# K and V caches loaded by groups of partitions instead of groups of heads

## The chip, the cores and the metric

The kernel runs on one core of one Trainium2 chip. The metric is the device time of one execution in microseconds. The kernel before took 277.62, 280.21 and 280.53 us in three runs, so its median is 280.21 us. The profile is of one more execution, of 279.63 us.

## The reference: what is computed

One decode step of an attention block beside a GEGLU feed-forward block, and its backward pass: the output and the gradients of x, both caches and all weights. The attention looks at the last W = 1024 positions of the caches only. Shapes: B = 4 sequences, one query position each, D = 512, 32 query heads, 8 kv-heads, a cache of 4096 positions, head size 128, F = 1792, all in bfloat16.

```python
xn = _layernorm(x)
q = (xn @ wq).reshape(B, 1, 32, 128).transpose(0, 2, 1, 3)
k = jnp.repeat(k_cache[:, :, Sk - W:, :], 4, axis=1)      # W = 1024 of Sk = 4096
v = jnp.repeat(v_cache[:, :, Sk - W:, :], 4, axis=1)
p = _softmax(jnp.einsum("bhqd,bhkd->bhqk", q, k) * 128 ** -0.5)
o = jnp.einsum("bhqk,bhkd->bhqd", p, v)
out = x + o.transpose(0, 2, 1, 3).reshape(B, 1, 4096) @ wo + (_gelu(xn @ w_gate) * (xn @ w_up)) @ w_down
# returned: out, and the vjp of it for grad_out in x, k_cache, v_cache, wq, wo, w_gate, w_up, w_down
```

The gradients of the caches have the full shape (4, 8, 4096, 128). Their first 3072 positions are zero, and the kernel has to write these zeros.

## The kernel before

**Memory traffic.** Of 111.88 MB that the DMA engines move, the loads into the on-chip memory SBUF (128 partitions) are 30.68 MB: the weights, and for each of the four sequences one K tile and one V tile of 2 MB. The stores are 81.01 MB. 32 stores of 1.5 MB write the zeros of the cache gradients, all from one constant tile `ztile` (function `zeros`, L278). The rest are results: 16 stores of 1 MB for the last 1024 positions of dK and dV, and the weight gradients.

**Queues.** Every load and every store of zeros is issued by SyncE (SP), in the order of the program; the transfers of one issuer form one queue (q1), which each of the 16 DMA engines works off in order. The result stores are issued by GpSimd (POOL) on a queue of its own (q0, function `result`, L113). `zeros(n)` lets at most four stores of zeros be under way at once. The compiled program also gives SP's transfers eight semaphores in turn, so a transfer waits to be issued until the one eight issues before it has landed.

**Order on SP's queue.** Weights; K of sequence 0; three stores of zeros; V of sequence 0; 2 zeros; K of 1; 4 zeros; V of 1; 2 zeros; K of 2; 3 zeros; V of 2; 2 zeros; K of 3; 3 zeros; V of 3; 13 zeros; two small outputs. K alternates between two buffers, `ka` and `kb`. V has a single buffer `va`, so V of sequence b + 1 is issued (L698) only when the matmuls of `od(0, b)` (L597) have read V of b. Below, K0 to K3 and V0 to V3 are the tiles of the sequences.

**How a tile lies.** `load_kv` (L258) makes a tile of [128 partitions, 8 kv-heads, 8, 128]. Partition m holds, of each kv-head, the positions 8m to 8m + 7 of the window. So for one partition and one head the source is a run of 8 x 128 x 2 = 2,048 bytes, and the heads lie 1 MB apart.

**Who reads a tile.** `score` (L528) transposes a tile on VectorE (DVE) in four steps of 128x1024 through `t32` (L92); each step reads all 128 partitions and every second kv-head (`src[:, g2:G:2, ...]`, L537), and matmuls on TensorE (PE, through `mm`, L136) follow. `score(0, b + 1, n)` for K of the next sequence is spread over the second half of the loop over b; `score(1, b, n)` for V of this one stands at its head. `od` (L597) then reads all partitions of the tile.

**The loop over sequences** (L643) holds the softmax, its backward pass and the matmuls for dK and dV (units of `dvdk`, L570, handed out by `move`, L121; their results go through `stg` tiles, L102, to the result stores). After it come the output projection (L737) and the weight gradients of wo and wq (from L749).

The calls of `load_kv` in the loop, with the zeros behind them (L697 to L699 and L718 to L720):

```python
                if b + 1 < B:
                    load_kv(b + 1, 1, att, "va", nc.sync)
                    zeros((2, 2, len(ztodo))[b])
...
                if b + 2 < B:
                    load_kv(b + 2, 0, (kap, att)[b % 2], ("ka", "kb")[b % 2], nc.sync)
                    zeros(3)
```

Of the kernel before, what the change touches and what calls it, by code (L numbers as in the profile page):

```python
# [15 lines left out]
P = 128  # L16
# [3 lines left out]
def kernel(  # L20
# [27 lines left out]
    _, G, Sk, Dh = A_k_cache.shape  # L48
# [4 lines left out]
    K0 = Sk - W  # L53
    F = B_w_gate.shape[1]
    Q = 32
# [5 lines left out]
    J = W // P  # L61
# [196 lines left out]
    def load_kv(b, k, pool, tag, eng, **kw):  # L258
        d_, src = ((k_t, A_k_cache), (v_t, A_v_cache))[k]
        tl = pool.tile([P, G, J, Dh], BF16, name=tag, tag=tag)  # L260
        for hf in range(2):
            hs = slice(hf * G // 2, (hf + 1) * G // 2)
            with tc.high_priority():
                d = eng.dma_start(out=tl[:, hs].rearrange("p g j d -> p g (j d)"),
                                  in_=src[b, hs, K0:Sk, :].rearrange("g (m j) d -> m g (j d)", j=J), **kw)
        d_[b] = tl
        return d

# [22 lines left out]
    if True:  # L291
# [15 lines left out]
        nc.sync.dma_start(out=wq_sb[:].rearrange("p c n -> p (c n)"), in_=A_wq.rearrange("(p c) n -> p (c n)", c=C))  # L307
        nc.sync.dma_start(out=wo_sb[:].rearrange("p k n -> p (k n)"), in_=A_wo.rearrange("(p k) n -> p (k n)", k=KH))
        load_kv(0, 0, kap, "ka", nc.sync)
        zeros(3)  # L310

# [117 lines left out]
    with tc.tile_pool(name="mid", bufs=1, reuse_waits="tile") as mid:  # L429
# [3 lines left out]
        selb = mid.tile([Q, 4, P], BF16, name="selb")  # L433
        with tc.tile_pool(name="att", bufs=1, reuse_waits="tile") as att:
            load_kv(0, 1, att, "va", nc.sync)
            zeros(2)
            load_kv(1, 0, att, "kb", nc.sync)
            zeros(4)

# [127 lines left out]
            def small(name, shape=(P, 1)):  # L567
                return att.tile(list(shape), FP32, name=name, tag=name)
# [74 lines left out]
            for b in range(B):  # L643
                S = sps[0][:]
                m = small("m")
# [249 lines left out]
```

## Time and profile before

| | |
|---|---|
| median of three runs | 280.21 us (277.62 to 280.53) |
| profiled execution | 279.63 us, its span 277.9 us |
| PE, DVE, ACT, POOL busy | 63%, 64%, 44%, 18% of the span |
| q1 (issued by SP) | 13,944 packets, 81.02 MB, 71.1% of 16 DMA engines' span |
| q0 (issued by POOL) | 6,368 packets, 30.67 MB, 27.2% |
| DMA parts of the chain that ended last | 30% of the span, 22% of it on `va` |
| `va` transfers, 1 MB each, issue to landing (median) | 14.6 us |
| `ka` and `kb` transfers, 1 MB each, issue to landing (median) | 24.5 and 21.6 us |
| stores of zeros, 1.5 MB each, issue to landing (median) | 20.9 us |

The span runs from the first instruction to the last. A share of DMA time adds the time that the packets took and divides it by 16 engines' span; packets of one engine overlap a little, so it can pass 100% in a short stretch. Time from issue to landing includes the wait behind older transfers of the same queue.

### The profile page before, as it was taken

The page shows a single profiled execution, that of the slowest core. Times are in us where ns is not written, and L with a number is a line of the kernel's source. Part 1 is how long each engine was busy: PE and PEld are TensorE (multiplying, and loading weights), DVE is VectorE, ACT ScalarE, POOL GpSimd, SP SyncE. Part 2 cuts the span into 40 slices and gives each one's busy share as a digit, 9 for nine tenths or more (in the row PEclk, how much of TensorE's full clock was granted, in tenths as well). Part 3 has the DMA queues.
Part 4 walks back from the last instruction along what each step waited for, and adds up shares of the span by engine and source line. Part 5 has one row for each costly group of instructions (what it writes and reads, how often), then busy time and mean ns, then how long its engine had stood idle before and what let it go on. Part 6 is the DMA issues. An engine that isn't in the chain of part 4 may idle for free.

```text
span 277.9 us, 3158 instructions
## 1 busy us (share of the span) xinstructions
PE 174.9 (63%) x1095; PEld 57.7 (21%) x1095; DVE 177.0 (64%) x331; ACT 122.0 (44%) x247; POOL 50.6 (18%) x121
## 2 busy tenths in 40 slices
PE   1257988868347857986430987631987366897560
PEld 0112432123023411331000323101332001122010
DVE  7789679889787198738321736713718376665980
ACT  2244676730202475847150644540646257353470
POOL 8500100285152013310200100200200202010110
PEclk9985985559755555575555555555555557555555
DMA  7999989999999999999999999999999999999686
GB/s 263 435 472 416 410 337 427 425 426 402 430 403 433 429 403 424 409 429 424 394 416 428 409 421 424 396 417 432 431 417 426 409 417 406 413 392 408 270 333 246
DMA packets 20335, 111.88 MB, mean 403 GB/s; under 512 B 1360, under 2 KB 1376, under 8 KB 14688
## 3 DMA queue, kind: packets, MB, share of 16 engines
q1 hardware_dynamic: 13944, 81.02, 71.1%
q0 software_dynamic: 6368, 30.67, 27.2%
q8 instruction: 8, 0.13, 0.2%
q14 instruction: 7, 0.06, 0.0%
q10 hardware_dynamic: 8, 0.00, 0.0%
HBM read 30.68 MB, written 81.01 MB: 402 GB/s over the span
## 4 chain that ended last, share of the span: by engine, by line
DMA 30%; PE 23%; DVE 9%; ACT 5%; issue 3%; SPq 0%; POOLq 0%; DVEq 0%; ACTq 0%
DMA va<-in_A_v_cache_dram 22%; DMA out_dram<-stg 9%; PE dw_ps L136 5%; DVE scr L94 5%; PE kv_ps L136 4%; ACT stg L119 3%; PE sc_ps L136 3%; PE od_ps L136 3%; PE dxq_ps L136 1%; PE dn_ps L136 1%; PE ob_ps L136 1%; PE es_ps L136 1%; PE gs_ps L136 1%; ACT E_f L663 1%; DVE stg L119 1%
## 5 line engine op out<-in xcount | busy, mean ns | idle before, releaser
L119 ACT CAST stg<-kv_ps 128x512 bf16<-128x512 f32 x116 | 61.6, 600 | 72.3 <-PE kv_ps L136 59.8
L107 POOL DMA_DIRECT2D out_dram<-stg x26 | 17.9, 689 | 162.3 <-ACT stg L119 115.3
L136 PE MATMUL sc_ps<-scr,bd 128*32 128x256 bf16 x256 | 19.8, 403 | 37.5 <-DVE scr L94 37.0
L136 PE MATMUL kv_ps<-qm,spr 64*128 64x512 bf16 x64 | 24.6, 596 | 12.4 <-ACT stg L119 12.4
L94 DVE STREAM_TRANSPOSE scr<-va 128x1024 uint32<-128x1024 uint32 x16 | 19.5, 1225 | 20.1 <-DMA va<-in_A_v_cache_dram 20.1
L119 DVE CAST stg<-kv_ps 128x512 bf16<-128x512 f32 x12 | 7.9, 687 | 26.7 <-PE kv_ps L136 15.4
L136 PE MATMUL kv_ps<-dyBD,spr 64*128 64x512 bf16 x64 | 21.4, 607 | 1.5 <-ACT stg L119 1.5
L136 PEld LDWEIGHTS <-bd 128*32 128x32 bf16 x256 | 6.4, 107 | 55.0 <-issue 54.2
L136 PEld LDWEIGHTS <-spr 64*128 64x128 bf16 (+1 forms) x192 | 8.9, 106 | 40.0 <-issue 36.8
L119 DVE CAST more<-dw_ps 128x512 bf16<-128x512 f32 x16 | 10.9, 684 | 6.5 <-PE dw_ps L136 6.4
L119 ACT CAST more<-dw_ps 128x512 bf16<-128x512 f32 x16 | 9.1, 586 | 13.4 <-PE dw_ps L136 13.4
L136 PE MATMUL dw_ps<-dqSP,xn_b 32*128 32x512 bf16 x32 | 10.1, 592 | 5.9 <-ACT stg L119 5.5
L89 ACT CAST stg<-dwg_ps 128x448 bf16<-128x448 f32 x26 | 11.8, 566 | 2.4 <-PE dwg_ps L136 1.4
L136 PE MATMUL do_ps<-scr,dyBD 128*128 128x512 bf16 x32 | 9.8, 441 | 3.8 <-DVE scr L94 3.6
L119 ACT CAST stg<-dw_ps 128x512 bf16<-128x512 f32 x16 | 9.1, 586 | 6.2 <-PE dw_ps L136 6.0
L615 DVE SCALAR_TENSOR_TENSOR odt<-od_ps,om,odt 128x128 f32<-128x128 f32 x12 | 4.2, 351 | 11.8 <-ACT odt L610 11.5
L119 DVE CAST stg<-dw_ps 128x512 bf16<-128x512 f32 x16 | 10.4, 682 | 1.6 <-PE dw_ps L136 1.4
L136 PE MATMUL dw_ps<-dy_b,oSP 32*128 32x512 bf16 x32 | 9.1, 600 | 3.3 <-DVE oSP L753 1.8
L526 POOL COPY bd<-D3d 32x64 bf16<-32x64 bf16 x32 | 6.9, 229 | 20.7 <-PE sc_ps L136 11.4
L94 DVE STREAM_TRANSPOSE scr<-ka 128x1024 uint32<-128x1024 uint32 x8 | 9.8, 1233 | 0.8 <-PE r_ps L136 0.8
L94 DVE STREAM_TRANSPOSE scr<-wo_sb 128x1024 uint32<-128x1024 uint32 x8 | 9.7, 1232 | 0.7 <-PE do_ps L136 0.6
L526 POOL COPY bd<-D3q 32x64 bf16<-32x64 bf16 x32 | 7.2, 238 | 15.7 <-DVE d L94 13.8
(202 smaller groups left out, 319.6 us busy)
## 6 DMA issues: line engine op xcount, KB each, us to landing
out_dram<-ztile SPq DMA_DIRECT2D x32, 1536.0 KB, 20.9
out_dram<-stg POOLq DMA_DIRECT2D x20, 1024.0 KB, 15.1
va<-in_A_v_cache_dram SPq DMA_DIRECT2D x8, 1024.0 KB, 14.6
out_dram<-stg POOLq DMA_DIRECT2D x6, 896.0 KB, 10.7
wq_sb<-in_A_wq_dram SPq DMA_DIRECT2D x1, 4096.0 KB, 23.4
wo_sb<-in_A_wo_dram SPq DMA_DIRECT2D x1, 4096.0 KB, 34.4
ka<-in_A_k_cache_dram SPq DMA_DIRECT2D x4, 1024.0 KB, 24.5
kb<-in_A_k_cache_dram SPq DMA_DIRECT2D x4, 1024.0 KB, 21.6
```

The lines of the kernel that those rows point to most:

```text
L89: return nc.scalar.copy(out=out, in_=in_)
L94: nc.vector.transpose(out=out, in_=in_)
L107: d = eng.dma_start(out=out, in_=in_, **kw)
L119: return nc.scalar.copy(out=out, in_=in_) if eng == "act" else nc.vector.tensor_copy(out=out, in_=in_)
L136: nc.tensor.matmul(out, lhsT=lhsT, rhs=rhs, start=first, stop=last, **kw)
L526: nc.gpsimd.tensor_copy(out=t_[q, :, :, g2, :, o_:o_ + 4], in_=src[q, b, g2])
L615: STT(out=t_[:], in0=ps[:, g, :], scalar=(om, oms)[k][:, g:g + 1], in1=t_[:], op0=ALU.mult, op1=ALU.add)
L663: nc.scalar.activation(out=E_f[:], in_=S, func=ACT.Exp, bias=negm[:, 0:1], scale=1.0, accum_out=es[:])
```

## The change

`load_kv` cuts a tile by partitions instead of by kv-heads. Before, each tile came by two transfers of 128 partitions x 4 kv-heads. After, K comes by two transfers of 64 adjacent partitions x 8 kv-heads (`P // 2` = 64) and V by four of 32 adjacent partitions x 8 kv-heads (`Q` = 32). The bytes of a tile, its place in SBUF and the runs of 2,048 bytes stay the same. SP issues 24 K and V transfers in place of 16. No other line is changed, and the order of the instructions on the other engines is the same.

```diff
-        for hf in range(2):
-            hs = slice(hf * G // 2, (hf + 1) * G // 2)
+        n = (P // 2, Q)[k]
+        for ms in (slice(m, m + n) for m in range(0, P, n)):
             with tc.high_priority():
-                d = eng.dma_start(out=tl[:, hs].rearrange("p g j d -> p g (j d)"),
-                                  in_=src[b, hs, K0:Sk, :].rearrange("g (m j) d -> m g (j d)", j=J), **kw)
+                d = eng.dma_start(out=tl[ms].rearrange("p g j d -> p g (j d)"),
+                                  in_=src[b, :, K0:Sk, :].rearrange("g (m j) d -> m g (j d)", j=J)[ms], **kw)
```

## The prediction

> **What bounds the kernel now.** I read the 40 slices of the page first, then the chain of waits, then VectorE's timeline where the chain runs through a load, and last the DMA traffic in short windows.
>
> ```profile
> DMA  7999989999999999999999999999999999999686
> GB/s 263 435 472 416 410 337 427 425 426 402 430 403 433 429 403 424 409 429 424 394 416 428 409 421 424 396 417 432 431 417 426 409 417 406 413 392 408 270 333 246
> ```
>
> From the second slice to the 37th (7 to 257 us) the 16 DMA engines are full at 390 to 435 GB/s, whatever else the kernel does. The chain shows where that becomes time:
>
> ```profile
> 119.87 0.37 SPq L264
> 120.30 31.29 DMA va<-in_A_v_cache_dram
> 151.71 1.26 DVE scr L94
> ...
> 162.00 0.37 SPq L264
> 162.42 29.47 DMA va<-in_A_v_cache_dram
> 192.01 1.26 DVE scr L94
> ```
>
> V2 and V3 are issued as soon as their buffer is free and land 31 and 29 us later (columns: start, us, what), because 2 MB of V stand behind K and the zeros already in SP's queue. VectorE's timeline has the wait that ends there in brackets; V1 has none:
>
> ```profile
> 109.48 1.23 DVE L94 STREAM_TRANSPOSE scr<-va 128x1024 uint32<-128x1024 uint32 x1
> ```
> ```profile
> 151.71 1.25 DVE L94 STREAM_TRANSPOSE scr<-va 128x1024 uint32<-128x1024 uint32 x1 [9.99 <-DMA va<-in_A_v_cache_dram]
> ```
> ```profile
> 192.01 1.25 DVE L94 STREAM_TRANSPOSE scr<-va 128x1024 uint32<-128x1024 uint32 x1 [10.15 <-DMA va<-in_A_v_cache_dram]
> ```
>
> So the end hangs on how soon the DMA engines have worked off everything ahead of V3. The queue never runs dry and its order is fixed, so a microsecond of DMA work added anywhere before V3's landing should come out as about a microsecond at the end; behind it come 86 us (192 to 278) that the change leaves alone. The packet records put the eight tiles at 36.4-49.3 (K0), 63.3-72.5 (V0), 77.4-84.9 (K1), 97.4-104.8 (V1), 110.4-124.7 (K2), 134.4-151.2 (V2), 153.5-164.5 (K3) and 172.1-191.5 us (V3). First use, by VectorE: 73.5, 80.8, 97.7, 109.5, 125.8, 151.7, 169.6, 192.0. V1 has 4.7 us to spare and K2 one; V2 and V3 have less than nothing.
>
> **What a load packet costs now.** Three windows of the DMA traffic: 88 to 92 us (stores of zeros alone), 80 to 84 (K1 with few zeros), 140 to 144 (V2 beside result stores).
>
> ```profile
> q1 hardware_dynamic: 156, 1.71, 100.4%
> ```
> ```profile
> DMA packets 680, 1.68 MB, mean 420 GB/s; under 512 B 29, under 2 KB 29, under 8 KB 646
> ...
> q1 hardware_dynamic: 680, 1.68, 108.4%
> ```
> ```profile
> q0 software_dynamic: 281, 1.09, 66.6%
> q1 hardware_dynamic: 279, 0.56, 35.9%
> ```
>
> A q1 row: packets, MB, share of 16 engines' time. In the first, 1.71 MB is 139 packets of 12,288 B, so one takes 1.004 x 64 us / 139 = 0.462 us: 26.6 GB/s per engine, at which 2,048 B would take 77 ns. In the second, 646 - 29 = 617 packets have 2,048 B and 34 are zeros; (69.4 - 34 x 0.462) / 617 = 87 ns for a load packet. In the third the engines take one POOL packet (4 KB, 163 ns) and one load packet in turn. So loads already run at the engines' own rate, and all 16 together at 420 GB/s.
>
> **Part by part.** *Removed: 16 transfers; added: 8 K transfers of 1 MB, 16 V transfers of 0.5 MB.* The packets stay 8 x 1,024 of 2,048 B. A gain from their time is bounded: from 87 ns to 77 would be 10 x 64 packets per engine = 0.6 us a tile, and they overlap already (108%), so I take nothing.
>
> *Eight more issues on SP*, 0.37 us at the least (the first V issue at 119.87): 3 us on SP's queue. They delay the zeros and the K behind each V, while work for 7 to 14 us stands ahead in the DMA queue (V1 was issued at 90.1 and its packets began at 97.4, V2 at 120.3 and 134.4); cost 0, at most 3 us without that cover. Each transfer waits for the one eight issues before it, and eight issues are now fewer bytes: at the least 2 K + 4 V + 2 zeros = 2.1 + 2.1 + 3.1 = 7.3 MB, or 17.6 us at 0.415 MB/us, so the queue stays fed. The tightest new wait is V3's fourth piece, behind the landing of K3's first half; K3 is through at 164.5, V3's packets start at 172.1. Behind that wait stand 13 stores of zeros: cost 0. VectorE's first transpose of a V tile waits on four semaphores in place of two, about 0.05 us each as in the chain's "DVEq L94 0.05" pieces: 0.4 us in all. No reader starts earlier, since every transpose and every `od` matmul reads all 128 partitions.
>
> *Where the bytes land* is the unknown. Before, the 16 engines together write all 128 partitions; after, all 16 write 64 adjacent partitions at once (K), or 32 (V). If every engine's way into SBUF is shared by the partitions it serves, half the partitions are half the ways. No load of before shows that. Nearest rows: above, loads over all partitions, 87 ns; below, the few loads into four adjacent partitions, of packets of 1,024 B: for `dy4` 44, 88, 44 and 44 ns, the doubled one starting while the first ran; for `x4` 46 ns each, two of them together. One row speaks for sharing, one against, both on packets that a buffer might swallow. So the cost of a load packet goes from 0 more to 2 x 77 - 87 = 67 ns more, that is 64 x 67 ns = 4.3 us per tile. I take the upper end, because a long run of packets fills any buffer, but only where two engines are in load packets together:
> - K1, V1, K3 run without POOL packets (0.12 MB of them at most): 3 x 4.3 = 12.9 us.
> - V0 has 0.71 MB of POOL packets of 7,168 B, about 100 beside 1,024: 3.9 us.
> - K2, V2, V3 have 2.30, 2.76 and 2.81 MB of POOL packets of 4,096 B, 561 to 686 of them; while an engine alternates 163 and 87 ns, two engines fit on one way (2 x 77 of 250 ns). The uncovered 45, 34 and 33% cost 1.9 + 1.5 + 1.4 us. K0, 2.57 MB in larger packets (about 340): 2.9 us.
>
> Sum 24.5 us. A tile's stretch also holds zeros of engines that run ahead or behind (0.96 MB beside 2.10 MB in K1 and in V1); an engine in zeros writes nothing to SBUF and frees the way. I take a quarter off: 18 us. V1's 4.7 us of slack hide nothing in the end, since all that stands behind V1 in the queue is as late as V1. 279.6 + 18 = 298, and about the same against the median of 280.2.
>
> [...]
>
> **The rivals.**
> - *Hidden*: the way into SBUF is not shared, or takes turns without loss. For it: the two `x4` packets. Against it: the doubled `dy4` packet. The time is 279.6 + 0.4 = 280.
> - *Uncovered*: the packets in alternation collide too, and no engine is out of step: 8 x 4.3 = 34 us, 314. Against it: the one-to-one alternation in the third window.
> - *Faster*: what lands last decides, and today the engines are out of step: V2's stretch holds 2.10 + 2.76 MB that must move and 1.94 MB of zeros, V3's 3.08 MB of zeros. At 0.415 MB/us these are 4.7 and 7.4 us in which some engines are done or not yet begun. Should the new spread of partitions over engines even them out, V2 and V3 land up to 12 us earlier, within the 10.0 + 10.2 us that VectorE waits; half of it gives 274. For it: short slices leave an engine less of its own to lag on. Against it: each engine's share of bytes is what it was. It decides if a load packet stays under 95 ns.
>
> **How the numbers follow.** Shared ways with cover (298): 0.57. Uncovered: 0.08. Hidden: 0.19, of which I count 0.04 as slower by small costs and 0.01 as faster. Faster: 0.16. Slower by over 1%: 0.57 + 0.08 + 0.04 = 0.69; within 1% (2.8 us, about what a measurement of this kernel can tell from no change): 0.14; faster: 0.17. The forecast's own range is 284 (a quarter of the sum) to 305 (nothing taken off); the range reaches up to 309, towards the uncovered case, and down to 276, past the hidden one to the near third of the faster one; it leaves out 0.11 below and 0.07 above.
>
> **What would show it.** In the changed profile the load packets of K1, V1 and K3 near 150 ns with DMA at 250 to 300 GB/s and still full in those stretches; VectorE waiting for V1 too; longer chain pieces on `va`. If the packets stay at 85 to 90 ns, the step of the shared ways is wrong; if they double and the time does not move, the step that every DMA microsecond before V3 counts is wrong.

## The result, and the profile after

The changed kernel takes 299.94 us (median of five runs, 297.64 to 300.2) against 280.21 us (five runs here, 277.62 to 281.73): the ratio is 1.0704, with a 95% interval of 1.0655 to 1.0754. The profiled execution took 297.64 us, 18.0 us more than the profiled one of before. Engine work is the same (VectorE busy 176.5 us, 177.0 before); the bytes are the same.

The 40 slices of the changed kernel's page, each now 7.4 us long, DMA share above and rate below:

```profile
DMA  7999999999999999999999999999999999999676
GB/s 284 434 452 422 339 355 351 424 426 265 346 310 303 432 414 370 377 303 345 424 410 399 383 345 394 410 418 414 409 415 419 425 413 427 411 398 418 269 315 257
```

The DMA engines are as busy as before, but in the slices with K and V loads (10 to 13 and 16 to 18) they move 265 to 377 GB/s. Full engines that move less: each packet takes longer. The DMA traffic from 88 to 92 us, nearly all of it K1, shows by how much:

```profile
DMA packets 446, 0.92 MB, mean 229 GB/s; under 512 B 14, under 2 KB 14, under 8 KB 443
...
q1 hardware_dynamic: 446, 0.92, 106.9%
```

446 - 14 = 432 packets, nearly all of 2,048 B, in 1.069 x 64 us are 158 ns each, where the 87 ns packets of before moved 420 GB/s. From 196 to 200 us V3 is loaded beside result stores:

```profile
DMA packets 480, 1.66 MB, mean 415 GB/s; under 512 B 30, under 2 KB 30, under 8 KB 463
...
q0 software_dynamic: 295, 1.13, 69.4%
q1 hardware_dynamic: 184, 0.52, 32.2%
```

Of q1's 0.322 x 64 = 20.6 us some 16 packets of zeros (480 - 463, less one of another queue) take 7.4. The other 13.2 us are 168 packets, or 138 if all 30 short ones are q1's: 79 to 96 ns each. With POOL packets between, the loss is nearly gone, and the rate is back at 415 GB/s.

The packet records say the same of all 8,192 load packets, sorted by how many of them are in flight in the middle of each one. With up to eight in flight a load packet of the changed kernel takes 90 ns on average (3,202 packets), with 15 or more 152 ns (2,613 packets). In the kernel before the two means are 86 and 85 ns. So the loss comes with many load packets at once, and only with the new cut.

VectorE's timeline at the first transpose of V1, V2 and V3:

```profile
122.73 1.25 DVE L94 STREAM_TRANSPOSE scr<-va 128x1024 uint32<-128x1024 uint32 x1 [14.72 <-DMA va<-in_A_v_cache_dram]
...
166.79 1.25 DVE L94 STREAM_TRANSPOSE scr<-va 128x1024 uint32<-128x1024 uint32 x1 [10.37 <-DMA va<-in_A_v_cache_dram]
...
210.32 1.25 DVE L94 STREAM_TRANSPOSE scr<-va 128x1024 uint32<-128x1024 uint32 x1 [10.85 <-DMA va<-in_A_v_cache_dram]
```

VectorE now waits for V1 too, and the waits for V2 and V3 are no shorter although everything has moved: V3's first use came at 192.0 us and comes at 210.3, 18.3 us later. From there to the end it is 85.6 us, 85.9 before. So the whole loss arises ahead of V3.

The chain of waits (start, us, what), where it goes through V2 and past V3's issue:

```profile
134.62 32.05 DMA va<-in_A_v_cache_dram
...
166.79 1.26 DVE scr L94
...
175.14 1.92 PE od_ps L136 x13
...
177.08 0.32 SPq L264
...
179.99 4.24 SPq L264
...
184.28 12.47 SPq L107
...
196.80 20.55 DMA out_dram<-ztile
```

The piece on V2 is as long as before (31.29 us); V2 only starts later. Behind V3's issue the chain no longer follows V3 but SP's issues and the stores of zeros queued there. With the DMA engines full everywhere, either path should lead to the end; this is argued, not shown.

### The profile page after: what moved, and what is told of

Read it like the earlier page. It is cut to its first block, busy times and chain, and to the rows that moved or that the text cites. A ratio compares the mean times of both kernels' runs of the same rounds, so it can differ in the third digit from the quotient of the medians.

```text
span 295.9 us, 3171 instructions
## 1 busy us (share of the span) xinstructions
PE 173.0 (58%) x1095; PEld 57.7 (20%) x1095; DVE 176.5 (60%) x331; ACT 121.9 (41%) x247; POOL 50.8 (17%) x121
## 4 chain that ended last, share of the span: by engine, by line
DMA 56%; SPq 21%; PE 10%; POOL 3%; ACT 3%; DVE 3%; issue 2%; POOLq 0%; ACTq 0%; DVEq 0%
DMA out_dram<-ztile 28%; SPq L107 17%; DMA va<-in_A_v_cache_dram 11%; DMA kb<-in_A_k_cache_dram 9%; DMA ka<-in_A_k_cache_dram 8%; SPq L264 4%; PE dw_ps L136 4%; ACT stg L119 3%; PE dxq_ps L136 1%; PE dn_ps L136 1%; POOL ztile L222 1%; DVE more L119 1%; PE od_ps L136 1%; PE out_ps L136 1%; POOL dyBD L245 1%
## 5 line engine op out<-in xcount | busy, mean ns | idle before, releaser
L107 POOL DMA_DIRECT2D out_dram<-stg x26 | 18.1, 697 | 167.2 <-ACT stg L119 116.2
L119 DVE CAST more<-dw_ps 128x512 bf16<-128x512 f32 x16 | 10.8, 682 | 6.4 <-PE dw_ps L136 6.4
L615 DVE SCALAR_TENSOR_TENSOR odt<-od_ps,om,odt 128x128 f32<-128x128 f32 x12 | 4.2, 351 | 11.8 <-ACT odt L610 11.5
L136 PE MATMUL dw_ps<-dy_b,oSP 32*128 32x512 bf16 x32 | 8.3, 533 | 3.4 <-DVE oSP L753 2.0
L94 DVE STREAM_TRANSPOSE scr<-kb 128x1024 uint32<-128x1024 uint32 x8 | 9.9, 1240 | 0.1
```

Of the source, the lines that this page charges most:

```text
L94: nc.vector.transpose(out=out, in_=in_)
L107: d = eng.dma_start(out=out, in_=in_, **kw)
L119: return nc.scalar.copy(out=out, in_=in_) if eng == "act" else nc.vector.tensor_copy(out=out, in_=in_)
L136: nc.tensor.matmul(out, lhsT=lhsT, rhs=rhs, start=first, stop=last, **kw)
L615: STT(out=t_[:], in0=ps[:, g, :], scalar=(om, oms)[k][:, g:g + 1], in1=t_[:], op0=ALU.mult, op1=ALU.add)
```

## The experiments

All times are medians, each with its ratio to the kernel before on the same chip and in the same session (279.5 to 280.0 us).

**The number of transfers.** V in four transfers as in the changed kernel, but all over 128 partitions:

```diff
-        for hf in range(2):
-            hs = slice(hf * G // 2, (hf + 1) * G // 2)
+        n = (G // 2, G // 4)[k]
+        for hs in (slice(h, h + n) for h in range(0, G, n)):
```

> All transfers span 128 partitions again; V comes by four transfers of two kv-heads, so SP issues as many transfers, and with the same eight-issue wait, as in the changed kernel. Theory of the shared ways into SBUF: load packets at 84 to 88 ns, time 280 us (ratio 1.00). Rival, the eight extra transfers and their waits cost the time: V's part of the loss stays, 286 us or more, with load packets at 85 ns and gaps in the DMA row.

Measured: 279.51 us, ratio 1.0002 (0.9976 to 1.0027). From 80 to 84 us the rate is 416 GB/s. Eight more issues, with their semaphores and the wait for the eighth issue before, cost nothing here.

**Spread partitions in place of adjacent ones.** The changed kernel with one line different:

```diff
-        for ms in (slice(m, m + n) for m in range(0, P, n)):
+        for ms in (slice(m, P, P // n) for m in range(P // n)):
```

> Two transfers of 64 partitions for K and four of 32 for V as in the changed kernel, but every second or every fourth partition in place of adjacent ones, on both sides. Theory of the shared ways: each transfer reaches all of them, so load packets return to 84 to 100 ns and the time to 280 to 284 us. Rival, 64 or 32 partitions in one transfer are slow whichever they are: packets near 150 ns where nothing covers them, 298 to 300 us.

Measured: 279.61 us, ratio 0.9998 (0.9969 to 1.0028). DMA traffic of this kernel from 80 to 84 us, nearly all K1:

```profile
DMA packets 731, 1.53 MB, mean 382 GB/s; under 512 B 24, under 2 KB 24, under 8 KB 723
```

Transfers of 64 and of 32 partitions, as many of them, in the same order: the loss is gone. With the same number of partitions in each transfer, what costs is that they are adjacent.

**Which side.** Two kernels read adjacent rows and write spread partitions, and the reverse:

```diff
-        for ms in (slice(m, m + n) for m in range(0, P, n)):
+        for i in range(P // n):
+            ms, to = slice(i * n, (i + 1) * n), slice(i, P, P // n)     # sbuf_strided
+            to, ms = slice(i * n, (i + 1) * n), slice(i, P, P // n)     # hbm_strided
...
-                d = eng.dma_start(out=tl[ms].rearrange("p g j d -> p g (j d)"),
+                d = eng.dma_start(out=tl[to].rearrange("p g j d -> p g (j d)"),
```

> As the changed kernel on the HBM side (64 or 32 adjacent rows are read), but written to every second (K) or fourth (V) partition. The rows of a tile then lie on other partitions than the reference has them, so K and V are paired wrongly; the work is the same. Theory of the shared ways into SBUF: only the written side matters, packets at 84 to 90 ns, 280 us. Rival, the order of the reads in HBM costs the time: 298 to 300 us.

> The opposite: every second or fourth row is read, and written to 64 or 32 adjacent partitions, with the same wrong pairing of K and V. Theory of the shared ways into SBUF: packets near 150 ns where nothing covers them and 298 to 300 us, as the changed kernel. Rival, the order of the reads in HBM: 280 us.

Measured: 279.7 us, ratio 1.0022 (0.9982 to 1.0062), with spread partitions in SBUF; 298.89 us, ratio 1.0664 (1.0591 to 1.0738), with spread rows in HBM. The two windows that hold K1, of the first kernel from 80 to 84 us and of the second from 88 to 92:

```profile
DMA packets 658, 1.61 MB, mean 402 GB/s; under 512 B 27, under 2 KB 27, under 8 KB 627
```
```profile
DMA packets 439, 0.89 MB, mean 223 GB/s; under 512 B 13, under 2 KB 13, under 8 KB 437
```

The rate follows the SBUF side alone. The order of reads in HBM is out as a cause.

**K alone, V alone.** `load_kv` with the new cut for one of the two and the old one for the other:

```diff
+        if k == 0:          # k_only; k == 1 in v_only
+            ...             # by partitions, as after
+        else:
+            ...             # by kv-heads, as before
```

> K by two of 64 adjacent partitions, V by two of four kv-heads as before. Every DMA microsecond before V3 counts: the K tiles' packets were lengthened by 2.1 + 4.0 + 3.4 + 1.6 = 11.1 us of each engine's time in the changed kernel, so 291 us (ratio 1.04). Rival, only V's transfers matter because the chain waits for V: 281 us or less.

> V by four of 32 adjacent partitions, K by two of four kv-heads as before. Every DMA microsecond before V3 counts: V's packets were lengthened by 4.1 + 1.6 + 0.9 + 0.2 = 6.8 us, so 287 us (ratio 1.025); with k_only the two losses add up to the change's 18 us. Rival, only V's transfers matter: 296 us or more.

Measured: 290.36 us, ratio 1.0374 (1.034 to 1.0407), and 287.05 us, 1.026 (1.0216 to 1.0304). The losses of 10.8 and 7.5 us add up to 18.3, near the change's 19.7. K counts although the chain of before does not name it: in one queue, a slow K delays the V behind it (V3's first use comes 10.0 us later with K alone). The slices of the K-only kernel show the four K tiles (slices 7, 12 and 13, 18, 24):

```profile
GB/s 278 434 465 432 327 377 305 428 423 407 429 255 332 427 408 428 413 226 384 428 409 427 408 226 414 427 410 429 429 422 422 432 425 427 411 413 407 391 341 221
```

One thing does not fit one for one. The mean load packet is 113 ns in the K-only kernel and 106 ns in the V-only one, 85 ns before. Times 512 packets per engine that is 14.4 and 10.8 us, more than the 10.8 and 7.5 us of time. The expectations took 11.1 and 6.8 us from the changed kernel; that they came near both times is luck, because longer packets than they took and a smaller effect per microsecond evened out. "Every microsecond before V3 counts", below, says where the rest went.

**64 or 32.** V by two of 64 adjacent partitions (`n = P // 2` for both):

> V by two of 64 adjacent partitions in place of four of 32, K as in the changed kernel. If 32 and 64 adjacent partitions reach the same ways, the same packets and 298 to 301 us. If 32 reach half as many as 64, V's packets get shorter here and the time falls by some us.

Measured: 300.06 us, ratio 1.0703 (1.0638 to 1.0768), no different from the change: 32 adjacent partitions do as badly as 64. Its load packets even averaged 130 ns, against 120 in the changed kernel; why is not known. Within the changed kernel the two lie as close: from 68 to 76 us, nearly all V0 by 32, the DMA engines moved 1.83 MB, 229 GB/s, which is the rate of K1 by 64 (88 to 92 us); V0's packets averaged 149 ns, K1's 148.

**64 across the middle.**

```diff
-        n = (P // 2, Q)[k]
-        for ms in (slice(m, m + n) for m in range(0, P, n)):
+        for ms in (slice(0, 32), slice(32, 96), slice(96, 128)):
```

> K and V by three transfers of 32, 64 and 32 partitions: 0 to 31, 32 to 95, 96 to 127. If it matters which half of SBUF the partitions lie in, the middle transfer takes 32 from each half and its packets stay at 84 ns; half the bytes are then slow, half the loss remains: 287 to 291 us. Rival, the number of adjacent partitions counts alone: all packets slow, 298 to 301 us.

Measured: 294.47 us, ratio 1.052 (1.0442 to 1.0597): less than the change, so the place of the partitions counts, but well over the 287 to 291 expected. DMA traffic from 84 to 88 us, in K1:

```profile
DMA packets 351, 0.69 MB, mean 172 GB/s; under 512 B 15, under 2 KB 15, under 8 KB 351
...
q1 hardware_dynamic: 351, 0.69, 106.6%
```

That is 1.066 x 64 us / 336 = 203 ns a packet, slower than the 154 ns (2 x 77) of the prediction's estimate for two engines that share. Engines still in the first transfer that hold up others already in the middle one would fit it; that was not tried by itself. The expectation's 84 ns for the middle transfer did not come in K1: taken in order of start, its 256, 512 and 256 packets averaged 122, 180 and 167 ns.

**16 partitions.** V by eight of 16, K as before (the V-only kernel with `n = 16`):

> V by eight of 16 adjacent partitions, K as in the kernel before. If 16 partitions reach half the ways of 32, four engines share one: uncovered packets near 4 x 77 = 308 ns, (308 - 87) x 64 = 14 us more for each of V0 and V1, some 5 to 8 us for V2 and V3, 305 to 320 us. Rival, 16 reach as many as 32: packets near 160 ns and 287 us as with V alone by 32.

Measured: 293.01 us, ratio 1.0466 (1.0383 to 1.0549). Worse than the 287.05 us of 32, so 16 adjacent partitions cost more, but not by the factor expected. DMA traffic from 68 to 72 us, V0:

```profile
DMA packets 320, 0.58 MB, mean 146 GB/s; under 512 B 35, under 2 KB 35, under 8 KB 320
...
q1 hardware_dynamic: 320, 0.58, 109.0%
```

1.09 x 64 us / 285 is 245 ns a packet, not 308. The eight slices follow one another, so engines out of step may lie in different slices and share less; that is argued only.

**The read side.** The kernel before, its zeros read from 64 adjacent partitions:

```diff
-    zsrc = bass.AP(tensor=ztile.tensor, offset=ztile.offset, ap=[[2 * ztile[:].ap[0][0], ZP], [0, ZG], [1, ZW]])
+    zsrc = bass.AP(tensor=ztile.tensor, offset=ztile.offset, ap=[[ztile[:].ap[0][0], ZP], [0, ZG], [1, ZW]])
```

> The kernel before with the zeros read from 64 adjacent partitions of the constant tile, not from every second one; loads untouched. If reads of SBUF share their ways as writes do, the 4,096 packets of 12,288 bytes go from 460 ns to some 920 where nothing covers them, up to 118 us of each engine's time: 340 us or more. Rival, only writes share: packets at 460 ns, 280 us.

Measured: 399.24 and 421.1 us in two executions; only the size is used here. The shorter is 119 us over the kernel before, where up to 118 us were expected. Zeros alone, from 104 to 108 us of the second:

```profile
DMA packets 90, 0.95 MB, mean 237 GB/s; under 512 B 13, under 2 KB 13, under 8 KB 13
...
q1 hardware_dynamic: 90, 0.95, 105.8%
```

77 packets in 1.058 x 64 us: 0.88 us each, 0.462 before. So reads from 64 adjacent partitions cost 1.9 times as much here, where writes to them cost 158 ns in place of 87, 1.8 times.

**What the end gains from less DMA work ahead of V3.** Two stores of zeros moved behind V3, then one alone (the first hunk only):

```diff
             load_kv(1, 0, att, "kb", nc.sync)
-            zeros(4)
+            zeros(3)
...
                     load_kv(b + 2, 0, (kap, att)[b % 2], ("ka", "kb")[b % 2], nc.sync)
-                    zeros(3)
+                    zeros((2, 3)[b])
```

> The kernel before with two stores of zeros (3.1 MB) moved from in front of V2 to behind V3; loads untouched. If every DMA microsecond before V3 counts and those behind it do not, the gain is 3.1 MB at 0.415 MB/us, 7.6 us: 272 us, and VectorE waits some 2 to 6 us for V2 in place of 10. Rival, the result stores of the tail then wait longer beside the zeros and give it back: 278 us or more.

> The kernel before with one store of zeros (1.57 MB) moved from in front of V1 to behind V3. V3 should land 3.8 us earlier. If what the end gains is limited by the result stores that drain beside the zeros (with two moved, the last store was issued 7.8 us earlier and drained 7.3 us longer), the gain is 0 to 2 us: 278 to 280 us. Rival, with one moved the tail still has room for it: 276 us.

Measured: 278.09 us, ratio 0.9934 (0.9902 to 0.9967), and 278.52 us, 0.9953 (0.9917 to 0.9988). Both beat the kernel before, by under 2 us. With two stores moved the 272 us expected did not come, and the rival (278 us or more) did; with one, the time lies in the 278 to 280 us expected. VectorE's timeline of the first, at V2 and V3, and the 40 slices of its page:

```profile
138.16 1.25 DVE L94 STREAM_TRANSPOSE scr<-va 128x1024 uint32<-128x1024 uint32 x1
...
183.14 1.25 DVE L94 STREAM_TRANSPOSE scr<-va 128x1024 uint32<-128x1024 uint32 x1 [9.75 <-DMA va<-in_A_v_cache_dram]
```
```profile
DMA  7999989999999999999999999999999999999991
```

V3 is used 8.9 us earlier (192.0 before), and VectorE's whole wait for V2 is gone, where 2 to 6 us of it were expected to stay. But the DMA engines are now full into the 39th slice. POOL's timeline at the last result store, before and with two stores of zeros moved:

```profile
271.70 0.53 POOL L107 DMA_DIRECT2D out_dram<-stg  x1 [2.12 <-issue]
```
```profile
263.91 0.53 POOL L107 DMA_DIRECT2D out_dram<-stg  x1 [2.12 <-issue]
```

It is issued 7.8 us earlier, but the last packet of a result store ends at 275.0 us, only 0.6 us earlier. The gain was given back to result stores that drain beside the zeros. There was little room for a gain: before, the two queues' packets took 71.1 and 27.2% of 16 engines' span, some 273 of 277.9 us, and another order does not make that work less.

## Why the prediction was right

**The forecast.** 298 us, measured 299.94. What the case "shared ways with cover" led one to expect came: packets to adjacent partitions took 158 ns with nothing beside them and 79 to 96 ns between POOL packets. The ways themselves are the author's explanation; no run shows them. The rival *hidden* fell with the 158 ns packets. *Uncovered* (314) fell with the time and with the short packets beside result stores. *Faster* fell: the stretches of V2 and V3 grew, from 16.8 and 19.4 us to 23.7 and 24.0, with 3.85 and 4.47 MB of zeros in them, so the engines were no more in step than before; and the kernel with spread partitions, with as many short transfers and packets of 87 ns, was no faster than before (279.61 us). Of the signs that were named, full DMA engines, VectorE's wait for V1 and K1's long packets (148 ns) came. V1's and K3's averaged only some 110 ns, and the chain's pieces on `va` did not grow (32.05 us on V2, 31.29 before; none on V3).

**The cost of a packet.** 67 ns more was forecast as the upper end; 158 - 87 = 71 ns was measured where nothing covers. That the SBUF side and adjacency cause it was argued from a doubled `dy4` packet, against two `x4` packets that spoke otherwise. The pair of spread kernels showed it: 279.7 us with spread partitions in SBUF, 298.89 us with adjacent ones. That a buffer might swallow short runs was an assumption that no run tested. The forecast charged V's packets, over 32 partitions, the same 67 ns as K's over 64, which no run of before shows; the changed kernel showed 149 ns for V0's and 148 for K1's, against 86 each before.

**The sum.** Over all 8,192 load packets the mean rose from 85.3 to 120.1 ns: 34.8 ns x 512 per engine = 17.8 us, where 18 stood in the forecast. By tile it came out otherwise:

| us per engine | K0 | V0 | K1 | V1 | K2 | V2 | K3 | V3 |
|---|---|---|---|---|---|---|---|---|
| forecast, before the quarter | 2.9 | 3.9 | 4.3 | 4.3 | 1.9 | 1.5 | 4.3 | 1.4 |
| measured | 2.1 | 4.1 | 4.0 | 1.6 | 3.4 | 0.9 | 1.6 | 0.2 |

The forecast read each tile's cover from where the tile lay before. The change itself moves the tiles: V1 came to lie at 106 to 122 us, beside 2.10 MB of result stores, K2 lost most of its 2.30 MB (0.41 left), and K3 ran beside 4.18 MB of zeros of engines out of step. The flat quarter taken off, for engines in zeros that leave the way free, was a guess that suited the sum; K1 and V0 show that it is wrong for a tile with nothing beside it. The cost of a packet was foreseen; that the sum came out so near was in part luck, because V1 and K3 were put too high, K2 too low, and these errors and the quarter evened out.

**Every microsecond before V3 counts.** It held for the change (17.8 us of packets, 18.0 us of time in the profiled executions) and its place was right: V3 18.3 us later, nothing behind it. As a rule it left out that the engines run out of step: those ahead work on stores of zeros queued behind V3 while others still load V3. How many bytes moved before V3 had landed is in the packet records (78.9 MB in the kernel before):

| | change | K alone | V alone | middle | V by 16 | all by 64 |
|---|---|---|---|---|---|---|
| load packets longer, us per engine | 17.8 | 14.4 | 10.8 | 13.7 | 17.5 | 22.9 |
| MB moved before V3 had landed | 79.1 | 77.4 | 77.2 | 78.0 | 77.4 | 77.9 |
| V3's first use later, us | 18.3 | 10.0 | 6.7 | 11.5 | 14.8 | 20.0 |

With K alone 1.5 MB less moved before V3 landed; at 0.415 MB/us that gives 3.6 of the 14.4 us back, and 10.8 are left. The same working gives 18.3, 10.8, 6.7, 11.5, 13.9 and 20.5 us for the six kernels, within 1 us of V3's delay in each. So it is the work done before V3's landing that counts, and part of what *Faster* hoped for does happen, against a larger loss. In the change about as many bytes moved before V3 had landed as in the kernel before, which the forecast had not worked out; that packets and time agreed one for one there was luck. Nor does a microsecond taken away come out at the end, as the moved zeros showed.

**Issues and waits at nothing.** Right, by the four V transfers over 128 partitions. The wait that the forecast named as tightest (V3's fourth piece) was not the longest. SP's timeline of the changed kernel, at V1:

```profile
90.22 10.16 SPq L264 DMA_DIRECT2D va<-in_A_v_cache_dram  x4
```

V1's third and fourth piece come eight issues behind the two halves of K1. The first half had landed by then; the fourth piece waits 1.8 us for the second, until 94.8 us. Most of SP's 10 us are the issuing instructions themselves, the fourth's 5.55 us above all, for which the profile shows no wait; issues of before take long too (4.05 us for the second half of K3). The DMA row reads 9 throughout: what was queued covered it. The page's chain now names SP with 21%, but 17 of these lie on the issues of zeros (L107) and only 4 on K and V (L264). That SP's part cost time is not shown by it, since as many issues over 128 partitions cost none.

## What to carry to other kernels

Try a transfer of 64 or 32 partitions with them spread (every second or fourth one) and not adjacent: here that made all of the 7% between the two kernels (279.61 us against 299.94), stores read from 64 adjacent partitions cost more too (0.88 us a packet in place of 0.462), and the number of transfers made no difference (279.51 us). In a kernel whose DMA engines are always full, price a transfer by the time of its packets and count everything that moves before the last load has landed, not only the load that the chain names. A price that depends on what runs beside it has to be read at the place where the work will lie, and a gain ahead of the last load must also find room behind it.

## What was not expected of the hardware

A packet of the other queue between two load packets seems to take away most of the loss: V3's load packets averaged 88 ns with 3.37 MB of result stores in their stretch, K1's 148 ns with none. No run took the result stores away from V3; the means by load packets in flight, in the section on the result, fit it. Packets far over the 154 ns estimated for two engines that share came too: with the transfer across the middle, 450 of 8,192 load packets took 200 ns or more, against 7 in the changed kernel; why is not shown.
